# Soft-capped attention and a squared-ReLU feed-forward on one core: a second batch with seven block products in its first matrix product, a bias summed on TensorE, and a new instruction order

## Chip, cores and metric

The kernel runs on one core of a Trainium2 chip. The metric is the device time of one execution in microseconds; the median of several runs counts. About 1% (6 us) is what a measurement can tell from no change.

## What is computed

The reference is attention with a soft cap (4 batches, 12 heads, 448 positions, head size 64), followed by a feed-forward block on its output, viewed as 1792 tokens of width 768:

```python
scores = cap * np.tanh(scale * q @ k.T / cap)
attn = softmax(scores);  x = (attn @ v) as [1792, 768]
h = x @ w_in                       # w_in is 768 x 2048
g = s * np.maximum(h, 0) ** 2 + b
out = g @ w_out                    # w_out is 2048 x 768
```

The weights `w_in` and `w_out` come as float64, so the kernel also turns them into 32-bit floats on the chip. Attention is computed in float32, the two large products in pairs of 16-bit floats (a high half and a low half): each float32 product becomes three 16-bit ones (high by high, high by low, low by high).

## The kernel before

The work is one long list of operations, split over five engines: TensorE (PE) multiplies, VectorE (DVE), ScalarE (ACT) and GpSimd (POOL) do the rest, SyncE (SP) issues all transfers. Every operation is registered once by `P.op` with a label, the engines that could do it, what it reads and what it writes. The string `ORDER` (line 120) then says in which order they are issued: a number is the place of the operation in the list, and a letter behind it (a, d, p) chooses ACT, DVE or POOL where there is a choice. I call such an entry a word. Each engine executes its own words strictly in that order, so an operation that waits holds up all later words of its engine. Buffers are taken from pools in the order of the words too.

For each batch the stages are:

- Attention, two heads at a time (`scores`, `pvs`): four float32 products for the scores of a block (line 422), tanh and exp on ACT (lines 437 and 441), sums of the exponentials partly on DVE or POOL (label `add`, helper lines 345 and 346), products with the values (line 492), then division and splitting of the result into halves (labels `norm`, `x_hi`, `x_lo`).
- Preparing weights: `win` and `wout` read float64 pieces, convert them (lines 632, 637, 641), find scales and split into halves. In `wout`, `omax` (line 361) takes the largest absolute value of a piece, `oamax` gathers them, and a one-column matmul called `lanes` (line 380) spreads the result over all partitions; PE waits for that. `csum` sums the rows of `w_out` for the bias term (b times the column sums of `w_out`): three additions of 128 x 512, then two more that fold 512 columns to 128, then one float32 matmul with a column of ones (`obias`, line 751).
- The first product. Batches 0 to 2 compute it directly in `products` (lines 827 to 829): for each of 16 blocks f of 128 output rows, 18 matmuls of 448 columns. Batch 3 alone is in `QUICK = (3,)` (line 113) and calls `quick` for each of the 8 pairs g of blocks instead. This is Strassen's scheme in Winograd's form: a 2 x 2 block product from seven block products rather than eight, each on half the columns, at the price of sums of blocks before and after.
- The second product. Batches 1 to 3 use seven block products too (`m2pair`, line 1055), batch 0 is direct (lines 1139 to 1141).

What `quick` costs on the other engines: the differences of blocks of x (`blocks`, label `lesx`, four subtractions for each of three pairs) and the splitting of those (`xe_hi`, `xe_lo`, 128 x 672); per pair g, seven block products of nine matmuls with 224 columns (line 968), a `snap` on ACT (line 978) that takes the first block product out of PSUM, and six additions on DVE (`joined`, label `plus`, line 930: four of 128 x 224 and two of 128 x 448), which read a block product from PSUM and add it to a running sum, and then ReLU and square in place. The mixed weights that it needs are made by `mixq`, 12 times (`qfull`, four subtractions at lines 803 to 806, `q_hi`, `q_lo`), stored to memory and loaded again (`loadq`, 512 KB each). `mix` does the same for the second product (`m_lo`, line 877, line 886 and so on). In the order before, none of the 12 `mixq` is issued ahead of the first product of batch 2; all must be done for that of batch 3.

The parts of `quick` that matter, with the seven block products each run as one operation of PE:

```python
for i, (a, b, wk, bk, end) in enumerate((
    (w(0, 0), x(0, 0), whole, xk(0), ()),
    (w(1, 0), x(1, 0), whole, xk(1), ((0,), (1,))),
    (sm(0, 0), ex(2), mixed, ek, ((1, 2), (1, 2))),
    ...
    pe(("m1p", j, g, i), mm, ...)
    if i:
        joined(("plus", j, g, i), kp, at, view, kR, end, sc, [("wc", g)])
```

Of the kernel before, what the change touches and what calls it, by code (L numbers as in the profile page):

```python
# [14 lines left out]
ALU = mybir.AluOpType  # L15
# [97 lines left out]
QUICK = (3,)  # L113
# [7 lines left out]
8 4 12 6 15 3 13 777 10 14 18 9 24 11 2 782 63 845 16 778 33 21 19 25 787 17 26 779 30 834 22 40 31 23 67 27 20  # L121
780 835 28 64 34 5 32 789 29 850 35 36 793 70 784 65 37 41 42 38 43 824 120 39 836 781p 71 892 79 788 68 73 847
852 45d 783 69 785 837 80 74 798 72 75 76 846 851 786d 77 848 794 800 66 840 853 803 849d 119 829 54d 44d 825 56
46 55 81 790 88 795 118 82 799 83 89 85 791p 792 90 47 78 801 796 887 95 134 91 805 84 802d 797d 86 804 831 841
92 806 100d 830 807d 893 897 838d 96 93 808 137 826 87 827 135 828d 121 138 832 97 854d 842 94 57 98 58 122 59
125 136 894 809 48 833p 839 810 109d 60 99d 123 843 126 895 844d 811 131 855 856 128 857 888 124 140 858 812d
861d 189 110 49 863d 127 139 101 190 867d 129 191 150 132 130 899 111 865d 151 247 862 820d 869d 864 102 814d
143 866 133 141 144 196 193 145 197 871 898 51 142 815 896d 146 61d 147 199 192 881 816d 198 870 868 152 153 148
876 112 113 859d 194 889 195 890 900 200 817 882 873 208 939 50 214 202 883 201 203 115 860 215 149 872 901p
155d 154d 165 166 216 249 209 205 813 204 156 874 221d 210 878 217 157 248 940 251 884 206 877 885d 252 257 207  # L130
879 222d 167 875d 211 880d 168 218 224d 103 258 886 223d 219 254 212 114 891a 928 213 266 902 255 918 821 253
225d 52p 250 903 267 260 261 229d 158 220 226d 259 904 905 263 919 912d 908d 272 227 104 256 941 264 279d 305
# [12 lines left out]
1063 294p 1443 429 985d 993 498 471d 302 569 962 1435d 994 1398p 496 472d 508 466 509 467 468 1444 1003p 473d
499 823 505 1429d 1418 1005a 1404p 500 353 986d 1062 1419 1484 1073 1445 1485 1067 504 1077 1072 1064 506 486d
1065 474p 301 501 420 1420 1074 511 517 1004 520 477d 1068 507 422 987d 430 475 1405p 431 1446a 510 432 518 1075
521 512 527d 476a 1069 519 1007a 434 570 1399d 1421 1008 1006 528d 513 1078 1009a 522 995p 295 1081d 1079 1001a
303p 523 1070 433 487 1080 514 576 1472 1010 1088 577 1486 1473 571 515 479 362 1474 246 478 423 516 1448 996
1089 530d 997a 1487 488 999a 585 988d 535a 304 0 1422p 998 1475 582 1090 489 490 627 586 1162 491 524 525 583  # L150
1488a 526 1093a 630 1082p 572 1423d 531d 1476a 1083d 989d 1091a 573 1000 529d 1002 1477d 480 1094 578 579 1454
237 1103d 1449 574 584 990 1095a 1455 492 1450 1105p 1092 1104 575 580 1012 1106 1099p 544a 1466 1436 1437 425
581 1172 1447d 363 435d 1084d 1097d 1098 1101a 587 532d 493d 1456 1451 591 1157 588 1096 1438 494 1163 594 533
1174 629 1164 589 534a 590 1167 1102 595 596 640 597 991 601d 536 598 599 1452a 1173 592 593 1439 1489d 600 631
1168 1453d 1175 641 604d 642 1169 646 545 1165 424 546 1176 1406 1158 1170 537 538 618a 632 647 1171 1407 1166
1467 1159 1160 1161 1408 1177p 633 1440a 1184 609d 1409 1457 1185 1468 1100 1178d 1085d 628 637 643 1186 1197a
1195a 1198 1179p 1441d 1201a 1202 1412 1196 364 638 1413 1199d 602d 1200 1460 1478 365 1410d 685 1187a 1414
1191d 1011 1479 1461 366d 481 1411d 634 644 1415 1193a 1469 605d 1416d 547 1470a 1462 635 1124 1192 1417d 649
636 606d 1480 1204 1189a 1126 1180d 1194 368a 376d 374a 548 1086 1490 1458a 482 1119 1125 370d 1491 539 1463 639
645 687 603d 371 1471d 1188 188 1087 607 1127 377 1464a 652 653 659d 1120 1190 540 541 542d 1114 654 1128 1481  # L160
1504 1505 1121 1122 1482a 1109 372d 660d 650 608a 1116 1111 1459d 1110 1115 1117 1465d 549 686 550 651 695 648
689 696 1203 1112 1494 1113 1508 1483d 690 620 619 1129d 1107 1506 662p 1118 1123 691 1507 1108 1136 1137 373
1492 1138 1130d 1509a 1028 426d 1145a 1493 663p 664d 1280 1153d 1141a 1142 1154 1139a 1146 1143a 1140 1149a 697
621 698 655 1147a 688 1029 1030 1144 661d 656 692 699 611 1495a 707 610 657 1151d 1131d 1220 483 693 710 694 708
1152 1031 375 665 658 704 701 666a 667a 1518 1181p 717d 551d 1018 1150 367 669 1222 1519 1148 1019 1522 702 1182
1520 1023 676a 1205 1013 622 1521 718d 612 1032 1020 369 1511 705 436 700 1024 719d 668 1155 678 706 709 1025
703 677 1015 613 1021 720d 1221 1014 1223 1512 615 711 1022 1207 721d 1026 1016 1183 1206 722d 1132d 1208 679
712 1215 1523a 723 713 1033d 1133d 1156 1513 1027 1017 1209 724a 1040 624 623 1515 614 484p 1514 725d 1034p 1041
# [59 lines left out]
def attention_moe_kernel(  # L228
# [12 lines left out]
    nc = tc.nc  # L241
# [5 lines left out]
    QF = NF // NQ  # L247
# [3 lines left out]
    P = Plan()  # L251
# [471 lines left out]
    def wout(d):  # L723
# [556 lines left out]
```

## Time and profile before

| | us |
|---|---|
| median of 3 runs | 608.28 |
| lowest and highest run | 606.42, 610.15 |
| the profiled execution | 609.78 |
| its span, first to last instruction | 607.9 |
| PE busy | 589.2 |
| DVE busy | 493.6 |
| ACT busy | 371.6 |
| POOL busy | 130.0 |

All rows below are from the profiled execution, whose span is 1.9 us shorter than its time. Matmuls are pipelined: the busy time of a single one is a model of its whole passage, and what counts is the distance from the start of one to the start of the next.

### The profile page before, as it was taken

To read this page: it belongs to the slowest core of one execution; us is meant where nothing else is said; L and a number is where in the kernel's file an instruction comes from. 1 tells how busy PE (TensorE), PEld (TensorE's weight loads), DVE (VectorE), ACT (ScalarE), POOL (GpSimd) and SP (SyncE) were. 2 spreads that over 40 slices of the span, in tenths; PEclk is the share of its full clock that TensorE was granted. 3 is DMA by queue.
4 is the path that set the end of the run, shared out by engine and by line. 5 is a ranking of instruction groups with operands and counts; after the bars stand their busy time and mean duration, and the time that the engine had idled before them with its cause. 6 is when DMAs were issued, how large, how long until landed. Compare 5 with 4: busy or idle time off the path is not lost.

```text
span 607.9 us, 11861 instructions
## 1 busy us (share of the span) xinstructions
PE 589.2 (97%) x4619; PEld 360.3 (59%) x4619; DVE 493.6 (81%) x979; ACT 371.6 (61%) x537; POOL 130.0 (21%) x121
## 2 busy tenths in 40 slices
PE   6999999999999998999999999999999999999997
PEld 2232222343444443344555589777558999999997
DVE  0689999989998899799998999889768857587522
ACT  6999998998898875753566873343355023345200
POOL 0100422005510103000011022011422141843500
PEclk9999999999999999999999999999999999999999
DMA  8948575287037265354628578755337567774762
GB/s 318 369 127 259 187 207 157 69 252 243 7 111 247 83 190 209 125 176 138 212 100 288 194 290 289 255 198 159 120 115 274 197 209 241 263 251 149 246 221 79
DMA packets 54967, 118.91 MB, mean 196 GB/s; under 512 B 12544, under 2 KB 28032, under 8 KB 54912
## 3 DMA queue, kind: packets, MB, share of 16 engines
q1 hardware_dynamic: 54912, 118.16, 57.7%
q8 instruction: 36, 0.59, 0.4%
q14 instruction: 19, 0.16, 0.1%
HBM read 93.59 MB, written 24.47 MB: 194 GB/s over the span
## 4 chain that ended last, share of the span: by engine, by line
PE 62%; DVE 19%; ACT 10%; DMA 5%; issue 3%; POOL 0%; SPq 0%; DVEq 0%; ACTq 0%; POOLq 0%
PE bank L1055 22%; PE bank L827 7%; PE bank L828 7%; PE bank L829 7%; DVE bed L345 5%; PE bank L968 5%; ACT bed L437 4%; ACT bed L441 3%; PE bank L422 3%; PE bank L492 3%; DVE bed L641 2%; PE bank L1139 2%; PE bank L1140 2%; PE bank L1141 2%; DMA bed<-in_kq 1%
## 5 line engine op out<-in xcount | busy, mean ns | idle before, releaser
L345 DVE TENSOR_TENSOR bed<-bed 128x224 f32<-128x224 f32 (+6 forms) x201 | 155.2, 795 | 23.1 <-PE bank L532 3.8
L1055 PEld LDWEIGHTS <-bed 128*128 128x128 f16 x1512 | 144.8, 98 | 2.7 <-DMA bed<-w 0.3
L346 POOL TENSOR_TENSOR bed<-bed 128x224 f32<-128x224 f32 (+7 forms) x63 | 76.7, 1229 | 247.8 <-ACT bed L1008 63.4
L828 PE MATMUL bank<-bed,w 128*128 128x448 f16 x288 | 101.8, 353 | 0.0
L827 PE MATMUL bank<-bed,w 128*128 128x448 f16 x288 | 101.3, 352 | 0.0
L829 PE MATMUL bank<-bed,w 128*128 128x448 f16 x288 | 100.9, 350 | 0.0
L437 ACT ACTIVATE bed<-bank,arena 128x896 f32<-128x896 f32 x84 | 82.2, 1007 | 11.1 <-PE bank L422 6.0
L1055 PE MATMUL bank<-gt,bed 128*128 128x224 f16 x864 | 88.7, 259 | 0.0
L930 DVE SCALAR_TENSOR_TENSOR bed<-bank,arena,bed 128x224 f32<-128x224 f32 (+1 forms) x102 | 52.1, 525 | 44.8 <-PE bank L1055 28.4
L441 ACT ACTIVATE bed<-bed,par 128x896 f32<-128x896 f32 x84 | 85.4, 1046 | 0.3
L422 PE MATMUL bank<-bed 64*128 64x448 f32 x288 | 68.4, 585 | 6.1 <-DMA bed<-in_kq 5.0
L1055 PE MATMUL bank<-bed 128*128 128x224 f16 x648 | 67.0, 259 | 0.0
L492 PE MATMUL bank<-bed 128*32 128x448 f32 x576 | 63.2, 545 | 1.8 <-DVE bed L475 0.9
L422 PEld LDWEIGHTS bank<-bed 64*128 64x128 f32 x288 | 24.8, 192 | 42.8 <-issue 17.9
L827 PEld LDWEIGHTS <-w 128*128 128x128 f16 x288 | 27.9, 97 | 30.9 <-issue 6.0
L1004 ACT ACTIVATE bed<-bank,arena 128x448 f32<-128x448 f32 x32 | 19.9, 629 | 41.0 <-PE bank L829 34.6
L829 PEld LDWEIGHTS <-w 128*128 128x128 f16 x288 | 28.4, 98 | 26.5
L356 DVE SCALAR_TENSOR_TENSOR bed<-bed,arena 128x256 f16<-128x256 f32 (+2 forms) x75 | 41.2, 567 | 1.4 <-ACT bed L337 1.3
L828 PEld LDWEIGHTS <-w 128*128 128x128 f16 x288 | 27.8, 96 | 24.3
L492 PEld LDWEIGHTS bank<-bed 128*32 128x32 f32 x576 | 15.4, 109 | 42.0 <-issue 27.3
L345 DVE TENSOR_TENSOR gt<-bed,gt 128x448 f16<-128x448 f32 x48 | 35.0, 737 | 4.1 <-ACT gt L337 2.0
L1078 ACT ACTIVATE bed<-bank,arena 128x224 f32<-128x224 f32 x18 | 8.9, 535 | 43.8 <-DMA out_dram<-bed 30.4
(129 smaller groups left out, 824.3 us busy)
## 6 DMA issues: line engine op xcount, KB each, us to landing
bed<-ws SPq DMA_DIRECT2D x36, 512.0 KB, 5.3
bed<-w SPq DMA_DIRECT2D x30, 512.0 KB, 4.7
bed<-in_w_out SPq DMA_DIRECT2D x24, 512.0 KB, 4.5
bed<-in_kq SPq DMA_DIRECT2D x24, 448.0 KB, 4.5
bed<-in_w_in SPq DMA_DIRECT2D x18, 512.0 KB, 5.5
bed<-in_v SPq DMA_DIRECT2D x24, 256.0 KB, 4.5
w<-bed SPq DMA_DIRECT2D x12, 512.0 KB, 5.0
ws<-bed SPq DMA_DIRECT2D x12, 512.0 KB, 3.9
```

Source lines behind the costliest of these rows:

```text
L345: "DVE": lambda: nc.vector.tensor_tensor(dst(), a(), c(), op),
L346: "POOL": lambda: nc.gpsimd.tensor_tensor(dst(), a(), c(), op),
L356: lambda: nc.vector.scalar_tensor_tensor(lo(), src(), sc, hi(), ALU.mult, ALU.subtract),
L422: nc.tensor.matmul(P[kp][:, h, 0:S], a[:, 0, c * 128:(c + 1) * 128], a[:, 1], start=True, stop=True)
L437: ("tanh", bb, c2, c), lambda: nc.scalar.activation(P[ke], P[kp][:, :, 0:S], AF.Tanh, scale=tsc[:, 0:1]),
L441: ("exp", bb, c2, c), lambda: nc.scalar.activation(P[ke], P[ke], AF.Exp, scale=par[:, 0:1]), r=["par"], w=[ke],
L492: nc.tensor.matmul(P[kp[x]][o, 0:S], P[kv[x]][:, c, o], P[kh[x][c]][:, h], start=not x and c == 0, stop=bool(x) and c == NC - 1,)
L827: nc.tensor.matmul(ps[:, 0:S], wh, x[:, 0], start=(c == 0), stop=False)
L828: nc.tensor.matmul(ps[:, 0:S], wh, x[:, 1], start=False, stop=False)
L829: nc.tensor.matmul(ps[:, 0:S], wl, x[:, 0], start=False, stop=(c == NP - 1))
L930: nc.vector.scalar_tensor_tensor(pick(to), ps, sc[:, 0:1], pick(of), ALU.mult, ALU.add)
L1055: nc.tensor.matmul(at(), w(g, zw), b(g, zb), start=g == 0 and x == 0, stop=g == n - 1 and x == 2,)
```

## The change

Three things differ. Batch 2 joins batch 3 in `QUICK`, so that its first product goes through `quick`. In `wout` the two folding additions go, and `obias` sums the four blocks of 128 columns by four accumulating matmuls. And the whole string `ORDER` is new, since the list now has 2446 operations in place of 2348; the sums of blocks themselves (`blocks`) are written as they were. Nothing else in the code changes.

```diff
-QUICK = (3,)
+QUICK = (2, 3)
...
 ORDER = """
-8 4 12 6 15 3 13 777 10 14 18 9 24 11 2 782 63 845 16 778 33 21 19 25 787 17 26 779 30 834 22 40 31 23 67 27 20
...
-2343 2344 2346 2278 2341 2342 2345 2347
+8 795 12 4 18 15 10 3 13 9 14 2 65 27 19 16 800 28 21 24 801 17 33 22 11 25 34 5 20 79 35 26 63 40 805 797 30 29
...
+2436 2444 2437 2441 2438 2439 2440 2442 2443 2445
 """
...
         kb = buf(("bps", d), "ps_m")
-        for n2 in (2, 1):
-            binary(
-                ("csum", d, 4 * n2), lambda n2=n2: P[kc][:, 0:n2], lambda n2=n2: P[kc][:, 0:n2],
-                lambda n2=n2: P[kc][:, n2:2 * n2], ALU.add, [], [kc],
-            )
-        pe(
-            ("obias", d), lambda: nc.tensor.matmul(P[kb][:, 0:1], P[kc][:, 0], one32, start=True, stop=True),
-            r=[kc, "one"], w=[kb],
-        )
+
+        def total():
+            for i in range(QF):
+                nc.tensor.matmul(P[kb][:, 0:1], P[kc][:, i], one32, start=i == 0, stop=i == QF - 1)
+
+        pe(("obias", d), total, r=[kc, "one"], w=[kb])
```

Counted by engine, the words of the order go from 805 to 825 for DVE, 536 to 579 for ACT, 112 to 111 for POOL, 375 to 387 for SP. DVE gains 48 `plus`, 9 `lesx` of batch 2 (and 2 of batch 3), 3 `xe_lo` and 9 `less` of batch 1, and gives away or loses 16 `csum`, 12 `x_hi`, 6 `g_hi`, 6 `g_lo`, 5 `e_lo` and some smaller ones. ACT gains 12 `x_hi`, 4 `xe_hi`, 5 `e_hi`, 8 `g_hi`, 8 `snap`, 6 of the copies out of PSUM in attention. Six of the 12 `mixq` now come ahead of the first block product of batch 2, the other six within that stage.

## Rows read from the trace of the kernel before

**Rows 1.** The page's first part: busy time, share and instructions by engine.

```profile
PE 589.2 (97%) x4619; PEld 360.3 (59%) x4619; DVE 493.6 (81%) x979; ACT 371.6 (61%) x537; POOL 130.0 (21%) x121
```

**Rows 2.** Busy time by stretch: stretch, length, engines' busy us (instructions), PE clock, DMA.

```profile
0.00:30.00 30.00, 23.95 (x164) 7.74 (x164) 11.08 (x23) 24.47 (x30) 3.09 (x13) 1.00 0.91 347
30.00:150.00 120.00, 115.22 (x943) 39.49 (x945) 113.38 (x232) 113.79 (x142) 24.89 (x11) 1.00 0.61 189
150.00:360.00 210.00, 206.60 (x1273) 97.47 (x1262) 191.80 (x405) 150.00 (x229) 31.21 (x25) 0.99 0.50 163
360.00:480.00 120.00, 119.96 (x970) 92.80 (x968) 100.46 (x176) 48.49 (x77) 26.95 (x29) 1.00 0.60 208
480.00:608.00 128.00, 123.44 (x1284) 122.77 (x1282) 76.84 (x146) 34.90 (x62) 43.91 (x44) 0.99 0.60 207
```

**Rows 3.** The chain that ended last, in order of time: start us, us, what.

```profile
236.82 2.48 DVE bed L345
...
354.89 17.25 PE bank L1055 x180
...
548.82 6.90 PE bank L968 x72
```

**Rows 4.** Timeline of PE at 327 us: start us, us, engine, line, operation, count.

```profile
327.33 0.17 PE L380 MATMUL bank<-brief,ones 128*128 128x1 bf16 x1
...
327.36 0.36 PE L751 MATMUL bank<-arena,bed 128*128 128x1 f32 x2
...
327.58 0.35 PE L827 MATMUL bank<-bed,w 128*128 128x448 f16 x1
...
327.77 0.35 PE L828 MATMUL bank<-bed,w 128*128 128x448 f16 x1
```

**Rows 5.** The instructions of line 751: count, shortest, median, longest ns, first and last start.

```profile
L751 PEld LDWEIGHTS bank<-arena,bed x12: 186/189/192, 182.2 to 335.8; 128*128 128x128 f32 x12
```

**Rows 6.** Timeline of PE at 32 us.

```profile
31.97 0.45 PE L685 MATMUL bank<-ones,bed 128*128 128x1 bf16 x12
```

**Rows 7.** Groups by line and shape: count, busy us, mean ns, idle before.

```profile
L930 DVE SCALAR_TENSOR_TENSOR bed<-bank,arena,bed 128x224 f32<-128x224 f32 x68 | 29.3, 447 | 25.8 <-PE bank L1055 12.9 <-ACT bed L978 6.3 <-PE bank L968 5.0
...
L345 DVE TENSOR_TENSOR bed<-bed 128x224 f32<-128x224 f32 x65 | 29.0, 467 | 6.7 <-POOL gt L346 3.4 <-ACT bed L1008 2.5 <-POOL bed L346 0.6
...
L930 DVE SCALAR_TENSOR_TENSOR bed<-bank,arena,bed 128x448 f32<-128x448 f32 x34 | 23.0, 682 | 19.1 <-PE bank L1055 15.5 <-PE bank L968 2.6
...
L345 DVE TENSOR_TENSOR bed<-bed 128x512 f32<-128x512 f32 x14 | 11.7, 835 | 0.0
...
L345 DVE TENSOR_TENSOR bed<-bed 128x256 f32<-128x256 f32 x6 | 2.5, 421 | 0.1
...
L345 DVE TENSOR_TENSOR bed<-bed 128x128 f32<-128x128 f32 x5 | 1.4, 284 | 0.0
```

**Rows 8.** Timeline of DVE around 368 us, and of PE.

```profile
367.44 2.39 DVE L345 TENSOR_TENSOR bed<-bed 128x672 f16<-128x672 f32 x3
...
370.82 0.93 PE L1055 MATMUL bank<-bed 128*128 128x224 f16 x8
```

**Rows 9.** Timeline of POOL, DVE and PE from 234 to 243 us (brackets: idle before).

```profile
234.23 5.39 POOL L346 TENSOR_TENSOR bed<-bed 128x896 f32<-128x896 f32 x3 [25.79 <-ACT bed L441]
...
235.27 1.55 DVE L345 TENSOR_TENSOR gt<-bed,gt 128x448 f16<-128x448 f32 x1
236.75 2.56 DVE L345 TENSOR_TENSOR bed<-bed 128x512 f32<-128x512 f32 x1
...
241.14 0.18 PE L380 MATMUL bank<-brief,ones 128*128 128x1 bf16 x1 [2.60 <-DVE brief L762]
...
242.07 0.58 PE L1139 MATMUL bank<-gt,bed 128*128 128x448 f16 x1
242.45 0.58 PE L1140 MATMUL bank<-gt,bed 128*128 128x448 f16 x1
```

**Rows 10.** Busy time from 241.4 to 244.8 us, columns as in rows 2.

```profile
241.40:244.80 3.40, 3.40 (x11) 1.36 (x10) 3.27 (x10) 1.78 (x4) 0.00 (x0) 0.50 0.00 0
```

**Rows 11.** All DVE operations of one form: shortest, median, longest ns.

```profile
L345 DVE TENSOR_TENSOR gt<-bed,gt x48: 574/618/2508, 149.5 to 565.8; 128x448 f16<-128x448 f32 x48
```

**Rows 12.** Waits: engine and line, waited for, us in total, times, longest.

```profile
DVE bed L930 <- PE bank L1055: 28.4, 19, 4.1
```

**Rows 13.** DMA issues: count, size, us to landing.

```profile
bed<-wq SPq DMA_DIRECT2D x12, 512.0 KB, 4.8
```

More of the change, by code (lines that the diff above doesn't have):

```diff
@@ new lines @@
+587 1453d 1083 361d 514 511 1089 501 1025a 1024 1026 1019a 475 515 1092 510 1479 476a 512 1020 1093 1015a 1006
+294d 603 517 1021a 1433 703 488 1007 504 351 1411d 516 520 1022 1486 527p 350 1487 1480 477d 1094 487 521 518
+1011a 1481 188 522 1084 1424 362 1100 1101 246 1095p 1102 1434d 1425 1482a 1490 519 600 1017a 1117a 513 1096d
+1111d 523 1016 524 525 1097d 352d 528d 478 424 526 1115a 434 1018 1028 1113a 295 535a 479 1107a 1435p 425 1118
+601 1426 604 1116 1109d 1108 1103d 1110 304 1098 1099 1172 1483p 1491 353 1105a 1177 597 598 530d 1106 1114 1492
@@ new lines @@
+689 1165 1527 375 709 1056 717 725 1286 735d 1214 718 1063a 1529a 1061d 1219 1215 722 1062 1064 675 1059a 723
+736d 1259 1057a 1060 737d 697 676 728 719 1216 1228 1217 690 706 726 576p 720 721 724 1145 634d 643d 1058 553
+738d 727 1517 1518 739d 1073 698 1519 1071a 1220 566d 740d 741 1221 742a 1223 1530 1507 1072 691 745 744 1230
+644 1069a 1222 699 754 729 1233p 730 1229 1224 1225 1065a 1231 1070 1226 1227 746 1067a 1232 731 1520 1234p 1538
+753 743a 1238 700 1235p 1239 755 694a 635 1068 1066 1240 692d 1255d 701d 747 1256 1260 1251a 1252 1241a 1556
@@ new lines @@
+1717 1516 1588d 1625d 1333 1631 1634 1636d 1589d 1626a 1665 1627d 1334 1335d 1635 1637a 1668 1638d 1350d 1502
+1669 1721 1646 1670 1666 1650 1337 1338d 1336 1647 1639a 1590a 1651 1591d 1351 1667 577a 567a 1352 1671 1673a
+1691 557a 1648 1652 579a 1340d 1672d 1695 1675a 1743 761 1641d 1353d 1727 1341 1339 1674d 1509 1537 1649 1653
+1640d 1654d 1676d 1655a 1683 1656d 559a 1657a 1716 1723 1677d 1659d 1696 1642d 1658d 1678d 1660d 580 578 1342
+1692 1694 1661d 1679d 581d 1643d 1343d 1345d 1354 582p 1693 1728 1720 1718 1344 1724 1725 1662a 1686 569a 1722
@@ new lines @@
+1697 1644a 1729 1730 1680a 1736 1739 1355d 1681d 1740 1733 1645d 1346 1663d 1726 1711 1356 1737 1731 1347 1348d
+1357 558 1734 1744 1684 1732 1685 1360p 1735 1738 1712 1707 1698 1741 1687 1704 1701 568 583d 1358d 1699 1708
+1750 1702 570 1705 1747 1365d 1749 560 1361 561d 1366 562p 1700 1782 1703 1362 1745 1748 1706 1349 1367 1742
+584a 1783 1709 1363p 1713 1368d 563d 1369 1755 1810 1759 1375d 1390d 1768 571d 1391 1746 1769 1756 1751 1765
+564a 565 1752 1376 1760 1758 572d 1392 1766 1843 1757 1762 585 1761 573d 1771 1393d 1377 1811 1378d 1763 574a
@@ new lines @@
+1872 1857 1874 1855 1374 1876 1804p 1900 1928 1398p 1878 1880 1882 1806d 1807d 1902 1898 1899 1912 1858 1388d
+1883 1885 1808a 1856 1860a 1897 1910 1809d 1904 1901 1906 1859d 1861d 1903 1862a 1394 1886 1884 1864d 1905 1907
+1908 1940 1909 1913 1911 1863p 1916 1888a 1865p 1938 1866p 1867d 1887d 1399 1890a 1934 1868d 1914 1929 1891d
+1999 1889d 1931 1892p 1932 1915 1893p 1933 1894p 1918p 1936 1935 1895a 1917 1389 1937 1959 1941 1939 794 1989
+1961 1957 1919a 1944 1896d 1958 1920d 1960 1921p 1956 1942 1923d 1922d 1924p 1925p 2017 1962 1963 1943 1965 1969
@@ new lines @@
+2261 2243 2263 2291 2244 2246 2198d 2249 2247 2262 2199p 2265 2250 2264 2248 2200d 2266 2320 2271 2201p 2267
+2321 2273 2268 2324 2270 2251d 2252a 2322 2274 2385 2111 2326 2328 2272 2277 2254p 2255d 2296 2253d 2353 2302
+2256d 2323 2325 2257p 2278 2275 2276 2258p 2279d 2259p 2327 2107 2332 2298 2294 2260d 2329 2300 2330 2333 2280d
+2352 2293 2396 2336 2382 2337 2381 2331 2349 2334 2339p 2361 2304 2295 2335 2297 2364 2299 2301 2282d 2305 2402
+2373 2357 2340d 2338d 2341a 2303 2306 2283p 2386 2307 2308 2281d 2284d 2389 2309 2417 2393 2310d 2313a 2342p
@@ L223 @@
+2314d 2413 2390 2358 2343p 2311p 2312d 2359 2394 2315d 2316d 2317p 2384 2374 2362 2344p 2391 2392 2351 2285p
+2399 2286d 2287a 2360 2395 2418 2363 2345d 2346d 2405 2347d 2367 2370 2387 2318d 2319d 2288d 2365 2354 2368 2397
[3 rows of a table added]
 """
```

168 lines of the change are left out of this document (70 added, 98 removed), and 4 rows, old and new, of the table ORDER.

## The prediction

> **What bounds the kernel now.** I read the engine totals first, then the busy time by stretch, then the chain of waits, then single timelines. PE is busy 589.2 of 607.9 us [rows 1]; since a matmul's busy time is modelled, I check it by the distance of starts. A product run of 224 columns goes at 17.25 us / 180 = 95.8 ns and 6.90 / 72 = 95.8 ns [rows 3], one of 448 columns at 327.77 - 327.58 = 0.19 us [rows 4]. So where PE is called busy in the feed-forward stages it really is at its pace. By stretch [rows 2], PE is idle 6.1 us in the first 30, then 4.8, 3.4, 0.0 and 4.6 us (the last is mostly the end, when the output is stored). Hence from 360 us on the time is PE's own work. Before 360 us DVE is nearly as full: idle 18.9 us in the first 30, when it has no data yet, then only 6.6 of 120 and 18.2 of 210. The two meet at the first block products of batch 1: DVE's last piece of data for the tail of a pair lands at 367.44 + 2.39 = 369.83 us, and the block product that reads it starts at 370.82 us [rows 8]. DVE has 1.0 us to spare there. So the kernel has two bounds: PE's sum, and DVE's work up to about 370 us.
>
> **The change, part by part.**
>
> *Seven block products for batch 2.* It removes 16 x 18 = 288 matmuls of 448 columns at 0.1892 us (two neighbours show 0.19 [rows 4]), 54.5 us, and adds 8 x 7 x 9 = 504 of 224 columns at 95.8 ns [rows 3], 48.3 us. PE's sum falls by 6.2 us. This lies in the stretch that is PE's alone, so nothing hides it.
>
> *What it adds on DVE.* 32 `plus` of 447 ns and 16 of 682 ns [rows 7] are 25.2 us, about 11 block subtractions of 467 ns 5.1 us. Against that, the new order takes 45 words and more off DVE (they are listed with the change), many of them to ACT, which is busy 48.5 of 120 us after 360 [rows 2]. Adding up all words by their mean durations, DVE ends at +6 us net, ACT at +27 us, POOL about even. In total that is hidden: DVE is idle 51 us from 480 on. What matters is when it is due. I added DVE's words, at 0.94 of their mean (neighbours overlap; the whole order then gives 486 against the 493.6 us of rows 1), up to the last piece for pair 1 of the second product of batch 1: 333 us before, 346 us after. PE's words up to the reader: 357 and 359. DVE's lead in work shrinks by 11 us, because `mix` and half of `mixq` come earlier; the spare 1.0 us [rows 8] doesn't cover it. What can is DVE's idle time ahead of there: 43.7 us, 18.9 of them at the start [rows 2], so 25 us in holes that longer queues of ready work can fill. If DVE fills 10 of these 25, PE waits nothing; if none, 10 us. The weight words depend on transfers alone, and so fit holes well; I take 3 us.
>
> *Waits behind.* A `plus` waits on DVE for PE's product; the second product already does so 19 times, 28.4 us in total [rows 12], and queued behind it stand the subtractions and splits that feed PE next. 48 more come in a stage whose DVE load was 100 of 120 us [rows 2]. I cost this at nothing, since PE itself runs on meanwhile, up to one stage's lead; it is part of the crowding above.
>
> *The 12 `loadq`* are 512 KB each, landing after 4.8 us [rows 13]. They and the stores of `mixq` stand on SP's queue ahead of later weight loads; the DMA share is 0.60 there [rows 2]. Cost nothing with that cover, at most one landing, 4.8 us, if a pair's three loads come late.
>
> *The bias.* Twelve small additions go: 421 ns and 284 ns each on DVE [rows 7], some 4 us with the one on POOL; it is work of DVE's full stretch, and counted above. PE gets three more float32 matmuls per `obias`. Each is two passes: before, the pair holds PE from 327.36 to 327.58 us [rows 4], 0.11 us a pass. 6 x 3 x 2 = 36 passes are 4.0 us. Bounds: a one-column 16-bit pass goes every 0.45 / 12, 38 ns [rows 6], giving 1.4 us; a float32 weight load takes 189 ns [rows 5], giving 6.8 us if nothing overlaps. I take 4.0, measured on the same form.
>
> *The order.* One loss in the old order is plain. Three POOL additions run from 234.23 to 239.62 us; beside them a subtraction and an addition on DVE take 1.55 and 2.56 us [rows 9], where their forms take 0.62 (median [rows 11]) and 0.84 us [rows 7]: 2.7 us lost. PE's `lanes` matmul hangs on that chain [rows 3] and waits 2.60 us [rows 9]. Then the granted clock falls to 0.50, the lower level of 1.2 GHz, for 3.4 us [rows 10], and 448-column matmuls come every 0.38 us instead of 0.19 [rows 9]: another 1.7 us. In the new order that `csum` is on POOL and the last words of DVE before the scale are `omax` reductions, which read one operand. I take 4.4 us as gained. Bounds: nothing, if the same collision happens elsewhere (bounded by the 8.2 us that PE idles between 30 and 360), or all of these 8.2 us.
>
> The Trainium skill, "SBUF — State Buffer", section "Who interferes with whom", says that DVE and GpSimd share one port pair as an exclusive lock: a DVE instruction with two SBUF inputs and a GpSimd one that reads SBUF block each other for a whole instruction. The 2.56 us of rows 9 and the longest 2508 ns against a median of 618 [rows 11] agree.
>
> Sum, against the profiled execution: 609.78 - 6.2 + 4.0 - 4.4 + 3.0 = 606.2 us. That execution lies 1.5 us above the median, so the forecast is 608.28 - 3.6 = 604.7 us.
>
> **The rivals.**
>
> *A, faster.* DVE fills its holes, and the additional `obias` passes fall where PE waited for data anyway: 608.28 - 6.2 - 4.4 + 0 to 4.0, that is 597.7 to 601.9, say 600. For it: PE idles 8.2 us between 30 and 360 [rows 2], and the longest single wait, that of rows 9, is a wait for data. Against it: the line 751 rows lie from 182 to 336 us [rows 5], where PE is busy 206.6 of 210.
>
> *B, slower: DVE becomes the bound before the block products of batch 1 and 2.* Price 10 us (11 less 1.0 spare), or more where POOL locks DVE: 608.28 - 6.2 + 4.0 + 10 = 616. It decides once the crowding passes 8.3 us without the gain of 4.4. For it: 1.0 us spare [rows 8], holes of 25 us in all. Against it: DVE words went to ACT, and POOL's did not grow. By the skill's rule each POOL word that overlaps a two-operand word of DVE adds up to its own length; in the block-product stage of batch 2 that would push the same way.
>
> *C, no gain: the passes cost a whole weight load.* 608.28 - 6.2 + 6.8 = 608.9, with no gain from the order. For it: 189 ns [rows 5]; against it: the 0.11 us a pass of rows 4, with two in a row.
>
> *D, the order doesn't do what it says*: it trades one stall for another. This is the forecast without the 4.4: 609, the same class as C.
>
> **How the numbers follow.** The forecast has 0.40, C and D together 0.14, A 0.33, B 0.13. Faster by over 1% (below 602.2) is A, 0.33; within 1%, which a measurement can't tell from no change, is the forecast with C and D, 0.54; slower (above 614.4) is B, 0.13. The range goes from the low end of A, 598, to B's threshold less a little, 613.
>
> **What would show it.** Right: the 504 matmuls of the first product's block form become 1008 at 95.8 ns with none of 448 columns for batch 2; `obias` at 0.9 us each; no PE gap over 1 us near the scales of `w_out`, and no half clock between 200 and 300 us; DVE busy near 500 us, ACT near 395. Wrong: PE idle in 330 to 420 us with DVE as the releaser (B), or PE idle before 300 us as large as now (D). The forecast is also wrong if block products of batch 2 go slower than 95.8 ns, waiting for PSUM that `plus` hasn't drained.

## The result and the profile after

The changed kernel took 613.82 us (median of 8 runs, 612.7 to 614.71) against 608.64 us for the kernel before (8 runs, 606.05 to 611.3): a ratio of 1.009, with the interval 1.0068 to 1.0111. It is slower by about 5 us, where the forecast said 3.6 us faster and its range ended at 613. That is 0.8 us beyond the range, and still within the 1% that the prediction called no change. The profiled execution took 614.71 us with a span of 612.6.

Up to line 745 nearly all line numbers of the new kernel are 4 higher than before, and from line 751 on 1 higher: the subtractions and low halves of line 345 stand at L349 (POOL's at L350), the direct first product at L828 to L830, `plus` at L931, the block products of the first product at L969 and of the second at L1056, the four subtractions of `mixq` at L804 to L807 and those of `mix` at L887 to L890; L878 is `mfull`, the word of `mix` that puts the two halves of a weight together again.

First the page's part 1, which answers [rows 1]:

```profile
PE 587.6 (96%) x4871; PEld 383.9 (63%) x4871; DVE 505.4 (83%) x999; ACT 396.4 (65%) x580; POOL 131.6 (21%) x120
```

DVE at 505 and ACT at 396 us are near the prediction's signs (500 and 395), though DVE rose by 11.8 us where its sum had 6. PE is busy 1.6 us less, and the span is 4.7 us longer: so it is PE's idle time that has grown. Where, the busy time by stretch says (columns as in [rows 2]):

```profile
0.00:30.00 30.00, 24.37 (x168) 8.07 (x172) 8.67 (x16) 24.20 (x29) 4.52 (x13) 1.00 0.72 269
30.00:150.00 120.00, 116.61 (x942) 39.23 (x937) 112.73 (x240) 115.84 (x148) 20.03 (x11) 1.00 0.64 200
150.00:360.00 210.00, 205.09 (x1273) 97.15 (x1266) 202.60 (x405) 162.73 (x243) 34.06 (x23) 1.00 0.58 191
360.00:480.00 120.00, 112.73 (x1163) 111.07 (x1161) 111.43 (x209) 60.59 (x103) 41.53 (x35) 1.00 0.66 234
...
330.00:360.00 30.00, 26.19 (x152) 14.60 (x151) 29.64 (x48) 22.01 (x33) 2.62 (x2) 1.00 0.64 222
360.00:460.00 100.00, 92.73 (x954) 91.07 (x952) 95.36 (x179) 46.81 (x78) 30.21 (x24) 1.00 0.68 242
```

The same two last stretches of the kernel before:

```profile
330.00:360.00 30.00, 30.00 (x188) 17.82 (x186) 28.64 (x53) 23.38 (x38) 2.98 (x3) 1.00 0.69 235
360.00:460.00 100.00, 99.96 (x762) 72.80 (x760) 84.33 (x146) 42.40 (x67) 22.84 (x25) 1.00 0.60 205
```

From 330 to 460 us PE idled 0.04 us before; now it idles 30 - 26.19 = 3.81 us up to 360 and 100 - 92.73 = 7.27 us after. DVE's share went up from 28.64 to 29.64 of 30 and from 84.33 to 95.36 of 100. These are the two places to explain; I call them the early and the late waits. Up to 330 us PE idles less than before: 5.63 + 3.39 + (4.91 - 3.81) = 10.1 us against 14.2 of [rows 2].

The chain that ended last, which answers [rows 3], runs on DVE up to 372 us and again in pieces up to 416 us; from 466 us it is almost only PE's product runs (start us, us, what):

```profile
346.89 0.61 DVE bed L887
...
348.98 0.69 DVE bed L890
349.67 2.51 DVE bed L349 x4
...
466.05 23.00 PE bank L1056 x240
...
563.32 46.02 PE bank L1056 x480
```

23.00 / 240 and 46.02 / 480 are both 95.8 ns: PE's pace is what it was.

**One early wait, read line by line.** ACT's timeline, then DVE's, then PE's, of the new kernel around 349 us (brackets: idle before, and what ended it):

```profile
344.33 0.62 ACT L1005 ACTIVATE bed<-bank,arena 128x448 f32<-128x448 f32 x1
346.92 0.76 ACT L341 ACTIVATE bed<-bed 128x672 f16<-128x672 f32 x1 [1.97 <-DVE bed L349]
349.70 1.06 ACT L895 ACTIVATE bed<-bed 128x1024 f16<-128x1024 f32 x1 [2.02 <-DVE bed L890]
350.67 0.56 ACT L1009 ACTIVATE bed<-bed 128x448 f32<-128x448 f32 x1
351.26 0.58 ACT L341 ACTIVATE gt<-bed 128x448 f16<-128x448 f32 x1
351.74 1.14 ACT L1005 ACTIVATE bed<-bank,arena 128x448 f32<-128x448 f32 x2
...
343.81 2.47 DVE L878 SCALAR_TENSOR_TENSOR bed<-bed,arena 128x1024 f32<-128x1024 f16 x2
346.21 0.68 DVE L349 TENSOR_TENSOR bed<-bed 128x224 f32<-128x224 f32 x2
346.81 0.68 DVE L887 TENSOR_TENSOR bed<-bed 128x512 f32<-128x512 f32 x1
...
348.98 0.69 DVE L890 TENSOR_TENSOR bed<-bed 128x512 f32<-128x512 f32 x1
...
349.94 0.35 PE L830 MATMUL bank<-bed,w 128*128 128x448 f16 x1
352.93 0.35 PE L828 MATMUL bank<-bed,w 128*128 128x448 f16 x1 [2.65 <-ACT bed L1005]
```

DVE has no gap; from 343.81 to 349.67 us it works on `mix`, with two block differences (L349, 0.68 us) in between. ACT stands idle twice: for 1.97 us in front of a splitting word (L341), which needs those two differences, and for 2.02 us in front of `m_hi` (L895), which needs the last of the four subtractions. Behind both in ACT's queue stands the ReLU (L1005) that takes PE's product out of PSUM. PE waits 2.65 us for room in PSUM. So the releaser that the page names is ACT, and the cause is DVE: ACT's own words ahead of the ReLU had been waiting for DVE.

**Two late waits.** First the longest, at 394 us: POOL's timeline, the chain on DVE (start us, us, what), and PE's timeline. Then POOL's, DVE's and PE's timelines around 411 us.

```profile
389.72 3.04 POOL L350 TENSOR_TENSOR bed<-bed 128x224 f32<-128x224 f32 x2 [6.83 <-DVE bed L349]
...
390.01 0.78 DVE bed L805
390.81 2.25 DVE bed L806
393.42 0.69 DVE bed L931
...
394.15 1.02 PE L969 MATMUL bank<-bed,w 128*128 128x224 f16 x9 [2.44 <-DVE bed L931]
...
407.79 2.98 POOL L350 TENSOR_TENSOR bed<-w 128x1024 f32<-128x1024 f16 x1 [15.03 <-DVE bed L349]
...
402.09 0.91 DVE L360 SCALAR_TENSOR_TENSOR bed<-bed,arena 128x672 f16<-128x672 f32 x1
...
408.69 2.78 DVE L360 SCALAR_TENSOR_TENSOR bed<-bed,arena 128x672 f16<-128x672 f32 x1
411.40 1.21 DVE L349 TENSOR_TENSOR bed<-w 128x1024 f32<-128x1024 f16 x1
412.54 2.67 DVE L931 SCALAR_TENSOR_TENSOR bed<-bank,arena,bed 128x448 f32<-128x448 f32 x5
...
413.26 1.89 PE L969 MATMUL bank<-bed,w 128*128 128x224 f16 x18 [1.65 <-DVE bed L931]
```

In both a `plus` (L931) is late. At 394 us subtractions of `mixq` (L805, L806) stand ahead of it, and two of them took 0.78 and 2.25 us beside two block differences on POOL, where the same two lines take a median of 0.43 us. At 411 us `qfull` of `mixq` (L349, 1.21 us) and a splitting word (L360) stand ahead of it; the splitting word took 2.78 us beside a POOL word of `mixq`, where one of the same form without POOL took 0.91 (at 402.09).

So collisions with POOL stand right ahead of these waits. Are they what is new? I added up what DVE's words lose beside POOL: of every word that overlaps one of POOL's and lasts over 15% longer than the median of its form alone, the excess. From 360 to 460 us that is 6.4 us in the changed kernel and 5.4 in the kernel before, where PE idled 0.04 us. The words themselves, without that excess, grew by 11 us. So the collisions are nearly as dear as they were; what has gone is the room that hid them. How much of the late waits would go if these POOL words were taken away, no run shows.

### The profile page after: what moved, and what is told of

Its sections match the earlier page's. It is cut to its first block, busy times and chain, and to the rows that moved or that the text cites. A ratio compares the mean times of both kernels' runs of the same rounds, so it can differ in the third digit from the quotient of the medians.

```text
span 612.6 us, 12461 instructions
## 1 busy us (share of the span) xinstructions
PE 587.6 (96%) x4871; PEld 383.9 (63%) x4871; DVE 505.4 (83%) x999; ACT 396.4 (65%) x580; POOL 131.6 (21%) x120
## 4 chain that ended last, share of the span: by engine, by line
PE 46%; DVE 38%; ACT 8%; issue 5%; DMA 2%; POOL 1%; SPq 0%; DVEq 0%; ACTq 0%
PE bank L1056 17%; DVE bed L349 14%; PE bank L969 10%; PE bank L426 4%; PE bank L496 3%; ACT bed L445 3%; ACT bed L441 3%; DVE arena L365 3%; DVE bed L931 2%; DVE bed L360 2%; PE bank L828 2%; PE bank L829 2%; PE bank L830 2%; DVE bed L878 2%; DVE bed L645 2%
## 5 line engine op out<-in xcount | busy, mean ns | idle before, releaser
L349 DVE TENSOR_TENSOR bed<-bed 128x224 f32<-128x224 f32 (+6 forms) x202 | 153.2, 783 | 2.6 <-DMA bed<-zd 0.6
L1056 PEld LDWEIGHTS <-bed 128*128 128x128 f16 x1512 | 144.9, 98 | 1.5 <-issue 1.3
L931 DVE SCALAR_TENSOR_TENSOR bed<-bank,arena,bed 128x224 f32<-128x224 f32 (+1 forms) x150 | 75.3, 525 | 63.1 <-PE bank L1056 25.8
L350 POOL TENSOR_TENSOR bed<-bed 128x224 f32<-128x224 f32 (+6 forms) x62 | 73.6, 1197 | 246.1 <-DVE bed L645 61.7
L441 ACT ACTIVATE bed<-bank,arena 128x896 f32<-128x896 f32 x84 | 82.9, 1010 | 12.8 <-PE bank L426 7.2
L1056 PE MATMUL bank<-gt,bed 128*128 128x224 f16 x864 | 89.3, 259 | 0.8 <-DVE bed L931 0.4
L828 PE MATMUL bank<-bed,w 128*128 128x448 f16 x192 | 67.5, 352 | 3.8 <-ACT bed L1005 3.8
L1056 PE MATMUL bank<-bed 128*128 128x224 f16 x648 | 68.1, 259 | 0.0
L829 PE MATMUL bank<-bed,w 128*128 128x448 f16 x192 | 67.8, 353 | 0.0
L830 PE MATMUL bank<-bed,w 128*128 128x448 f16 x192 | 67.2, 350 | 0.0
L969 PE MATMUL bank<-bed 128*128 128x224 f16 x576 | 60.2, 259 | 2.0 <-ACT bed L979 1.5
L969 PEld LDWEIGHTS <-bed 128*128 128x128 f16 x576 | 55.2, 97 | 2.5 <-issue 2.5
L341 ACT ACTIVATE bed<-bed,arena 128x256 f16<-128x256 f32 (+2 forms) x61 | 34.8, 598 | 26.6 <-DVE bed L349 15.4
L969 PE MATMUL bank<-bed,w 128*128 128x224 f16 x432 | 47.3, 258 | 4.9 <-DVE bed L931 4.3
L360 DVE SCALAR_TENSOR_TENSOR bed<-bed,arena 128x256 f16<-128x256 f32 (+2 forms) x78 | 47.1, 628 | 0.1
L969 PEld LDWEIGHTS <-w 128*128 128x128 f16 x432 | 41.4, 97 | 5.7 <-issue 5.6
L350 POOL TENSOR_TENSOR gt<-bed,gt 128x448 f16<-128x448 f32 x22 | 26.4, 1206 | 79.9 <-ACT gt L341 70.5
L988 ACT ACTIVATE bed<-bed 128x448 f32<-128x448 f32 x32 | 17.6, 569 | 39.7 <-DVE bed L931 39.4
```

The costliest lines, as they stand in the source:

```text
L349: "DVE": lambda: nc.vector.tensor_tensor(dst(), a(), c(), op),
L350: "POOL": lambda: nc.gpsimd.tensor_tensor(dst(), a(), c(), op),
L441: ("tanh", bb, c2, c), lambda: nc.scalar.activation(P[ke], P[kp][:, :, 0:S], AF.Tanh, scale=tsc[:, 0:1]),
L828: nc.tensor.matmul(ps[:, 0:S], wh, x[:, 0], start=(c == 0), stop=False)
L829: nc.tensor.matmul(ps[:, 0:S], wh, x[:, 1], start=False, stop=False)
L830: nc.tensor.matmul(ps[:, 0:S], wl, x[:, 0], start=False, stop=(c == NP - 1))
```

## The experiments

Besides times I use one number worked out from all rows of PE: its **stall**, the sum over neighbouring matmuls of the distance between starts beyond the form's own pace (95.8 ns for 224 columns, 0.19 us for 448, and so on). What is left of the distances is PE's own **work**. Both are of the one profiled execution of a kernel, and time that PE spends at the lower level of its clock counts as stall. The absolute value hangs on the pace taken for the matmuls of attention, which start in groups; what counts is the difference between two kernels. Before: 582.2 us of work and 17.2 of stall; after: 580.3 and 23.7.

**Mixing without its subtractions.** Three kernels leave out the four subtractions of each `mixq`, of each `mix`, or of both (a one-column addition stands in their place, so that the waits stay as they are; the mixed weights are then not the ones the product needs).

```diff
-            nc.vector.tensor_tensor(a22, a21, a22, ALU.add)
-            nc.vector.tensor_tensor(a21, a11, a21, ALU.subtract)
-            nc.vector.tensor_tensor(a11, a22, a11, ALU.subtract)
-            nc.vector.tensor_tensor(a12, a12, a11, ALU.subtract)
+            at = P[kf][:, 0, 0, 0:1]
+            nc.vector.tensor_tensor(at, at, at, ALU.add)
```

> The changed kernel without the four block subtractions in each of the 12 mixq (left out: the mixing of the first product's weights; a one-column addition stands in their place). 12 x 1.5 us of DVE work go, 6 of them before the first block product of batch 2. Theory (DVE's work that is due by about 445 us is the bound; PE waits 13 us between 330 and 460 us): those waits that lie behind mixq, 391 to 437 us, some 6 us, vanish, and the time falls to 605 to 609 us. Rival (the order itself is worse, or PE's own sum and psum turnover set the time): no change, 613 to 614 us.

> The changed kernel without the four subtractions in each of the six mix stages (left out: the mixing of the second product's weights). 6 x 2.8 = 17 us of DVE work between 290 and 355 us go. Theory (DVE is the bound from 290 us on): the two waits at 343 and 350 us, 4.1 us, vanish, and all that is queued behind comes earlier, so also most of the later ones: 602 to 606 us. Rival (the late waits come from mixq or batch 2's additions alone): only the 4.1 us go, 609 to 610 us. Rival (order or PE's own sum): 613 to 614 us.

> Both of the above: neither mix nor mixq subtracts. Theory: PE waits for nothing from 330 us on; PE's own sum and the early waits are left: 613.8 - 12 to 13 = 601 to 602 us, which is under the kernel before. Rival (order or PE's own sum): 613 to 614 us.

| kernel | us | ratio to before, interval | PE idle 330 to 360 | PE idle 360 to 460 | DVE busy 330 to 460 |
|---|---|---|---|---|---|
| before | 608.64 | | 0.00 | 0.04 | 113.0 |
| after | 613.82 | 1.009 (1.0068 to 1.0111) | 3.81 | 7.27 | 125.0 |
| without `mixq`'s subtractions | 608.41 | 1.000 (0.9977 to 1.0023) | 3.53 | 1.94 | 107.9 |
| without `mix`'s subtractions | 609.3 | 1.0011 (0.9991 to 1.0031) | 0.00 | 6.78 | 120.2 |
| without both | 603.71 | 0.9936 (0.9914 to 0.9958) | 0.00 | 1.94 | 105.5 |

The two rows of the kernel without both:

```profile
330.00:360.00 30.00, 30.00 (x198) 19.02 (x197) 25.22 (x48) 25.81 (x41) 1.08 (x1) 1.00 0.72 244
360.00:460.00 100.00, 98.06 (x1019) 97.32 (x1017) 80.30 (x152) 48.60 (x82) 36.26 (x31) 1.00 0.69 244
```

The subtractions of `mix` on DVE are 18.2 us in all (5.0 + 4.9 + 4.2 + 4.1), those of `mixq` 22.4 (6.9 + 5.4 + 5.1 + 5.0). With both gone, PE's work is the same (580.1) and its stall is 13.0 instead of 23.7. The early waits go with the subtractions of `mix` and stay without those of `mixq`; of the late ones 5.3 of 7.27 us go with those of `mixq`, and 0.5 with those of `mix`. Of these three, the first came out as expected; the second landed at the rival's number, because I had put more of the waits down to `mix` than the early ones; the third gave 603.71, 2 us above what I had expected: 1.94 us of late waits don't go away.

**Batch 2's first product direct again.** This is the changed kernel, order included, with only the first product of batch 2 put back.

```diff
-QUICK = (2, 3)
+QUICK = (3,)
...
-                kp = buf(("m1", j, g, i), "ps_s")
+                kp = buf(("m1", j, g, i), "ps_h" if j == 2 else "ps_s")
```

In the order the words of the direct product (PE's and the ReLU's) take places among those of batch 2's block products, and its `lesx`, `xe_hi`, `xe_lo`, `loadq`, `snap` and `plus` go.

> The changed kernel with the first product of batch 2 taken back to plain matmuls of 448 columns, everything else in the changed order (the mixtures of the weights and their transfers still stand early, and the new bias). PE's own work rises by 6.2 us to 586.5. Theory (the early mixtures and what they push late on DVE cost PE the waits between 330 and 430 us): the waits at 343 and 350 us (about 4) stay, since nothing before 360 us changes; of the later ones (about 9) those go that batch 2's own block differences and additions cause, so the stall falls by 2 to 8 and the time is 611 to 617 us. Rival 1 (batch 2's own differences and additions are what fills DVE): nearly all 13 us of waits go, 606 to 608. Rival 2 (the waits are the order's, whatever the words): stall as in the changed kernel, 23.7, and the time is 619 to 621.

Measured: 615.04 us (ratio 1.0101, 1.0067 to 1.0135), PE's work 586.4, stall 18.7. By stretch:

```profile
330.00:360.00 30.00, 26.47 (x139) 13.91 (x138) 29.65 (x49) 21.90 (x34) 2.64 (x2) 0.94 0.66 226
360.00:460.00 100.00, 99.77 (x779) 74.64 (x777) 71.92 (x131) 41.20 (x66) 27.80 (x22) 1.00 0.55 200
```

The early waits stay (3.53 us), as the theory says; the late ones are gone (0.23 us), and DVE drops to 72 of 100 us there. So the late waits need both: the subtractions of `mixq` in this place, and batch 2's block products with what hangs on them (48 `plus`, block differences, `snap`, `loadq`, which this run takes away together). Without the first 1.94 us stay, without the second 0.23. And the whole of the seven block products is worth little in this order: 6.1 us less of PE's work and 5.0 us more of stall leave 1.1 us. By the medians it is 615.04 - 613.82 = 1.2 us, which isn't clear of noise, since the two intervals overlap. The 5.0 is a net sum, too: the stall of 18.7 holds 1.7 us of lower clock behind the wait at 350 us, which the profiled execution of the changed kernel doesn't have.

**More of DVE's work in the kernel before.** In the other direction: eight of the `m_lo` words (1.22 us each) are done twice in the kernel before.

```diff
+                if p < 2:
+                    binary(
+                        ("m_lo2", p, e, x), lo, lambda f=kf[x]: P[f], hi, ALU.subtract, [kf[x], (ka[x], 0)], [(ka[x], 1)]
+                    )
```

> The kernel before with the eight low halves of mix pairs 0 and 1 computed twice on DVE (same values): 8 x 1.22 = 9.8 us more DVE work between 305 and 359 us, nothing else. Theory (DVE's due work is the second bound, with 1.0 us to spare at 370 us and about 4 us of holes from 300 us on): 609.3 + 5 to 9 us, 614 to 618 us. Rival (PE's own sum sets the time, the slower order of the changed kernel is its fault): no change, 609 us.

Measured: 614.45 us (ratio 1.0093, 1.0056 to 1.013), stall 21.5 instead of 17.2, PE idle for 3.25 us from 330 to 360 and 1.48 from 360 to 460, where the kernel before idled 0.04. The longest wait, 2.0 us, is again one for the ReLU on ACT, as in the changed kernel at 349 us. So the kernel before was that close to DVE's bound: 9.8 us more on DVE cost 4.3 us of stall.

**The bias alone.** In the kernel before, with `obias` as four matmuls and the twelve folding words gone:

```diff
-        for n2 in (2, 1):
-            binary(
-                ("csum", d, 4 * n2), lambda n2=n2: P[kc][:, 0:n2], lambda n2=n2: P[kc][:, 0:n2],
-                lambda n2=n2: P[kc][:, n2:2 * n2], ALU.add, [], [kc],
-            )
...
-            ("obias", d), lambda: nc.tensor.matmul(P[kb][:, 0:1], P[kc][:, 0], one32, start=True, stop=True),
...
+        def total():
+            for i in range(QF):
+                nc.tensor.matmul(P[kb][:, 0:1], P[kc][:, i], one32, start=i == 0, stop=i == QF - 1)
+        pe(("obias", d), total, r=[kc, "one"], w=[kb])
```

> The kernel before with the new bias sum alone: twelve small additions taken out of its order, four matmuls in each obias. PE's sum rises by 3.9 us, DVE's falls by 4 us. In this order PE itself is the bound from 300 us on and DVE has 1.0 us to spare at 370 us, so the theory of two bounds expects PE's 3.9 us to show, less 1 us for the wait at 238 us that DVE reaches earlier: 611 to 613 us against 609.3. Rival (the exchange of PE for DVE work is a gain in any order, DVE being the bound): 605 to 609 us.

Measured: 613.67 us (ratio 1.0092, 1.0064 to 1.0121); PE's last matmul ends 608.4 - 604.6 = 3.8 us later with the same stall in sum (17.1). The median is 0.7 us above the theory's range and far from the rival's: the passes show in full. That what DVE sheds brings nothing is less clear, for the equal stall is a net sum. The wait at 241 us stays (2.75 us), but in this execution the clock doesn't fall behind it; and from 480 to 540 us PE idles 2.33 us instead of 0.94, of which 1.3 us are a wait for a weight transfer that the kernel before doesn't have.

**The old bias in the changed kernel**, twice: with the two folding words of each piece just ahead of `obias` in the order, and with them right behind the piece's last `csum`, on the engine that did it.

> The changed kernel with the old bias sum: the two folding additions on DVE just ahead of each obias, and one matmul instead of four. PE's sum falls by 3.9 us, DVE's rises by some 4 us, three to five of the six pairs ahead of 340 us. Theory (DVE is the bound): the time rises by 0 to 4 us, 614 to 617 us. Rival (PE's own sum sets the time): it falls by 3.9 us, to 610 us.

> The changed kernel with the old bias sum, the two folding additions right behind the last of the three larger ones on the same engine (four of six on DVE, two on POOL) and one matmul. PE's sum falls by 3.9 us, DVE's rises by 4 x 0.7 = 2.8 us, all ahead of 300 us. Theory (DVE is the bound between 290 and 445 us, and PE's matmuls before that lie in its shadow): 613 to 617 us, that is no gain from PE's 3.9 us. Rival (PE's own sum sets the time): 610 us.

The first is a miss of mine: 625.88 us (ratio 1.03), 12 us above the changed kernel. The place in the order did it. Its waits of PE between 150 and 360 us, and PE's timeline of one of them:

```profile
PE bank L747 <- DVE bed L341: 12.1, 5, 3.0
...
226.15 0.56 PE L747 MATMUL bank<-arena,bed 128*128 128x1 f32 x2 [2.69 <-DVE bed L341]
...
223.00:232.50 9.50, 6.81 (x25) 2.39 (x23) 8.41 (x14) 5.69 (x9) 2.21 (x2) 0.64 0.25 80
```

The folds stand at the end of DVE's queue of that moment, so each `obias` (L747) waits up to 3.0 us for them, and after the wait the granted clock is at the lower level for a while (a mean of 0.64 over 223 to 232.5 us). The second, with the folds where they belong, took 615.15 us (ratio 1.0099, 1.0077 to 1.012): PE's work is 3.9 us less, its stall 3.7 us more (27.4). That is the theory's number, and the rival's 610 isn't. How the stall came back is not what the theory had said: up to 460 us PE idles only 1.4 us more, and most of the rest is lost in 6.8 us at the lower level of the clock:

```profile
354.40:357.80 3.40, 3.40 (x11) 1.41 (x10) 3.30 (x6) 2.45 (x5) 0.00 (x0) 0.50 0.52 205
395.30:398.70 3.40, 3.40 (x21) 2.65 (x19) 3.37 (x7) 1.36 (x3) 0.00 (x0) 0.50 0.00 0
```

That neither the passes saved nor the lower clock moves the time fits a stage that DVE sets: PE's wait for `snap` ends at 439.08 us here and at 438.68 in the changed kernel.

**One letter in the kernel before.** The `csum` that collided with POOL at 236 us [rows 9] goes to POOL.

```diff
-1129d
+1129p
```

> The kernel before with one letter of its order changed: the addition that took 2.56 us on DVE beside POOL's (csum of block 3, first) goes to POOL, behind the additions that run there. Theory: PE's wait of 2.60 us at 238 us shrinks to some 0.3 us and the 3.4 us at half clock vanish: 4 us, so 604.5 to 606 us against 609.3. Rival (DVE has 1.0 us to spare at 370 us, so PE only waits later): 608 to 609 us.

Measured: 606.28 us (ratio 0.9954, 0.9923 to 0.9984), PE's stall 13.5 instead of 17.2. PE's `lanes` matmul (L371 here) waits 0.64 instead of 2.60 us, and the clock stays at its upper level:

```profile
238.29 0.18 PE L371 MATMUL bank<-brief,ones 128*128 128x1 bf16 x1 [0.64 <-DVE brief L753]
...
237.00:242.00 5.00, 4.36 (x25) 2.09 (x24) 4.79 (x13) 1.33 (x3) 3.69 (x3) 1.00 0.31 105
```

The stall fell by 3.7 us, the time by 2.8 (0.0046 of 608.6). The median lies 0.3 us above the theory's range, on the theory's side of the rival's; the rows are the theory's, and all six executions show a mean granted clock of 1.000. One letter makes this kernel a little faster than the one before (the interval leaves out 1, though the gain is under 1%), and so faster than the changed one.

**DVE's words to the idle POOL.** In the changed kernel 19 block differences of the second product (128 x 224) go from DVE to POOL, between 300 and 430 us.

```diff
-1618d
+1618p
...
-1600d
+1600p
...
-1643d
+1643p
```

> The changed kernel with 19 of the block differences (128 x 224 float32 subtractions of two operands, 443 ns each on DVE, 790 ns on POOL) between about 300 and 430 us moved from DVE to POOL, which is idle nearly all of that time. DVE sheds 8.4 us of words there. Theory (DVE is the bound there and a two-operand word of POOL holds up DVE's two-operand words for as long as it lasts): no gain or a loss, 612 to 618, with DVE's words beside POOL's longer than their form's mean. Rival (DVE is the bound, but the two run freely side by side): 5 to 8 us less, 606 to 609.

Measured: 616.8 us (ratio 1.0124, 1.0066 to 1.0181), stall 26.4. DVE's groups from 300 to 440 us in this kernel, and POOL's:

```profile
L869 DVE SCALAR_TENSOR_TENSOR bed<-bed,arena 128x1024 f32<-128x1024 f16 x10 | 14.0, 1431 | 0.2
L340 DVE TENSOR_TENSOR bed<-bed 128x224 f32<-128x224 f32 x20 | 10.8, 543 | 0.1
...
L922 DVE SCALAR_TENSOR_TENSOR bed<-bank,arena,bed 128x224 f32<-128x224 f32 x23 | 9.5, 446 | 0.7
...
L341 POOL TENSOR_TENSOR bed<-bed 128x224 f32<-128x224 f32 x24 | 25.1, 1061 | 67.5 <-ACT bed L1000 48.0 <-DVE bed L340 6.8 <-DVE gt L340 4.3
```

The same DVE groups in the changed kernel:

```profile
L349 DVE TENSOR_TENSOR bed<-bed 128x224 f32<-128x224 f32 x40 | 16.8, 443 | 0.1
L878 DVE SCALAR_TENSOR_TENSOR bed<-bed,arena 128x1024 f32<-128x1024 f16 x10 | 12.9, 1318 | 0.0
L931 DVE SCALAR_TENSOR_TENSOR bed<-bank,arena,bed 128x224 f32<-128x224 f32 x25 | 10.3, 446 | 0.7
```

20 differences are left on DVE, at a mean of 543 instead of 443 ns; `mfull` takes 1431 instead of 1318. The means mix words beside POOL and words alone: 16 of the 20 take their 0.38 us, and the other four 0.73 to 2.31. By the sum of what DVE's words lose beside POOL, from 300 to 450 us that is 14.5 us here and 7.7 in the changed kernel. So DVE's busy time there falls only from 145.6 to 144.4 us, though 19 words have left it (8.4 us by the mean, 7.3 at 0.384 us alone). The theory holds and the rival's 606 to 609 doesn't; of the stall that is new, 1.7 us is lower clock behind the wait at 354 us. The Trainium skill, "SBUF — State Buffer", section "Who interferes with whom", calls the port pair that DVE and GpSimd share an exclusive lock; the trace agrees. `plus`, which reads one of its two operands from PSUM, takes 446 ns in both kernels, with POOL busy or not.

## Why the prediction was wrong

The sums of the prediction come out, but for one: in A, 608.28 - 6.2 - 4.4 + 4.0 is 601.7, not 601.9. Nothing hangs on it.

**Right: the block products and the bias.** PE's work fell from 582.2 to 580.3 us, by 1.9 where -6.2 + 4.0 = -2.2 was forecast. The 1008 block products of the first product go at 95.8 ns each, 96.6 us. `obias` takes 5.1 us in all instead of 1.2, so +3.9; one of them holds PE for 338.55 - 337.74 = 0.81 us (forecast 0.9):

```profile
337.74 0.95 PE L752 MATMUL bank<-arena,bed 128*128 128x1 f32 x8
338.55 0.35 PE L828 MATMUL bank<-bed,w 128*128 128x448 f16 x1
```

Rival C's weight load of 189 ns [rows 5] is hidden behind the pass before.

**Right: the order, up to 330 us.** The stall up to 330 us went from 15.2 to 9.9 us, 5.3 us where 4.4 were forecast. Between 200 and 300 us no half clock is left, and PE is busy the whole time:

```profile
200.00:300.00 100.00, 100.00 (x650) 45.65 (x649) 94.54 (x207) 73.54 (x112) 19.02 (x13) 1.00 0.58 191
```

The one-letter kernel shows that the mechanism was read rightly: the collision of [rows 9] alone is worth 3.7 us of stall. Rival D falls. That 5.3 lies so near 4.4 is in part luck: it is the net of many waits that the new order moved, and the 1.7 us of half clock in the forecast is a loss that not every execution of the kernel before shows (see the end).

**Wrong: DVE's crowding.** This is the step that failed, and in it one term: what queues up on DVE behind the 48 additions of batch 2, of which the prediction says "I cost this at nothing", came to 8.7 us of stall. In all, "I take 3 us" was 12.8: the stall from 330 to 460 us went from 0.2 to 13.0 us. The experiments separate the two parts.

1. Up to the first block products of batch 1 (the early waits) the price was nearly met: 4.1 us where 3 were taken. DVE filled holes much as reckoned: its idle time ahead of 360 us went from 43.7 to 21.3 + 7.3 + 7.4 = 36.0 us, 7.7 less, where 3 us of waits stood for 7 filled. But the path was another, and so the near hit is luck. The reader that was reckoned with, a block product of batch 1 at 370 us, hardly waits (0.3 us for its data). The 4.1 us came earlier, at 343 and 350 us, at direct products that found no room in PSUM, because `mix` stands in the same 20 us as the ReLU path of batch 1: its six stages of subtractions start between 293 and 347 us, where before they started between 302 and 387. A total over 370 us doesn't say which 20 us are full.
2. Behind that point (the late waits) the failing term stands: "48 more come in a stage whose DVE load was 100 of 120 us", costed at nothing. There I took PE's lead as cover. The stage's own sum, which I didn't make, has no room: of 120 us DVE had 19.5 to spare [rows 2]. In the trace 46 more `plus` start there (67 against 21, 24 us more), and the subtractions of three more `mixq` (11 against 8, 7.3 us more), against two fewer of `mix` (5.5 us less). Even with what was moved away, DVE is now busy 111.43 of 120 there, and PE idles 7.27. The experiments without `mixq`'s subtractions and with batch 2 direct each take this away, the first but for 1.94 us.

There is a smaller miss beside it: DVE's whole rise was put at 6 us and was 11.8. The sum went by mean durations of the kernel before. What DVE's words lose beside POOL, summed as above over the whole kernel, rose from 27.1 to 32.9 us; the prediction names this push under rival B and gives it no price.

Rival B had this mechanism, its place ("PE idle in 330 to 420 us with DVE as the releaser") and nearly its price: 10 us by its own reckoning against 12.8. With the gain up to 330 us against it, the time still stayed under B's 614.4. What spoke against B, "DVE words went to ACT, and POOL's did not grow", was true and didn't decide: ACT took 12 us more in the stretch from 360 to 480 us (60.59 against 48.49), and DVE still rose there by 11; and that POOL is nearly idle from 300 to 400 us is no reserve, as the experiment with 19 words on it shows.

**The sum, corrected.** Work -1.9, stall up to 330 us -5.3, from 330 to 460 us +12.8, behind it about -1.0: +4.6 us, and the profiled spans differ by 612.6 - 607.9 = 4.7 us.

**What stays open.** How much of the early waits could be had back by another place of `mix` alone, with everything else as it is, wasn't tried. Nor was taking the POOL words away that stand ahead of the late waits. That 1.94 us of late waits stay when all subtractions are gone wasn't followed further either; the trace puts 1.5 of them down to `snap` on ACT.

## What to carry to other kernels

When a change takes work off the engine that bounds a stage and puts work on a second one that is nearly full there (DVE was at 84% from 360 to 480 us and at 95% from 330 to 360), make the second engine's sum for each stage that the added work falls in, not only up to the first deadline: here one stage had 1.0 us to spare and the next 19.5 of 120, and the block products took 6.1 us off one engine for a net of some 1. An idle third engine is no reserve if it blocks the second: price the words it would take by how long both run side by side. And a reader that is shown as waiting for engine X should be followed one word further back in X's queue; here ACT was named, and DVE was the cause.

## What the runs showed that I had not expected

- The same edit has two prices. Four float32 matmuls for the bias instead of two folds and one cost 5 us in the kernel before (3.8 between the profiled executions), where PE is the bound at that place, and nothing in the changed one, where undoing them gave 615.15 against 613.82.
- Two words per `obias` in the wrong place of DVE's queue cost 12 us: 5 waits of up to 3.0 us, with the lower level of the clock after them.
- The same wait has different consequences for the clock. The wait of 2.65 us at 349 us is also in the kernel with batch 2 direct, at the same place and of the same length. In the profiled execution of the changed kernel the granted clock stays at its upper level behind it; in the other one it is at the lower level of 1.2 GHz for 3.4 us, which the mean of 0.94 from 330 to 360 us shows. It differs between executions of one kernel, too: of the 44 executions of the kernel before that stand beside the experiments, 30 have a mean granted clock of 0.994 to 0.997 and 14 of 0.999 to 1.000, and the medians of their spans are 607.5 and 605.5 us. In the changed kernel three executions of eight have 0.997, and their spans (610.6 to 612.0) are no longer than those of the other five (611.1 to 612.6). So one profiled execution doesn't say whether a kernel has this loss.
- Moving 19 words off the full engine, 7.3 to 8.4 us of work, lengthened its other words so much that its busy time fell by only 1.2 us.
